# Value sums in the rotating PSUM banks, and ScalarE as a second copier, in an attention-plus-MLP kernel

## The chip, the cores and the metric

The kernel runs on one core of a Trainium2 chip. The metric is the device time of one execution in microseconds (us), as the median of several; lower is better. The five engines are called as in the profile: PE (TensorE, matrix products), DVE (VectorE), ACT (ScalarE), POOL (GpSimd) and SP (which issues most DMAs). "The skill" below always means the Trainium skill, named with the page.

## The reference, cut to what matters

```python
x = A_x                                      # (1, 2048, 512), bf16
xn = _layernorm(x)
return x + attention(xn, wqkv, wo) + mlp(xn, w_gate, w_up, w_down)

# attention: 32 heads of 16; causal, window of 256 keys
scores = einsum("bhqd,bhkd->bhqk", q, k) * (Dh ** -0.5)
p = softmax(where(mask, scores, -1e9));  o = einsum("bhqk,bhkd->bhqd", p, v);  o @ wo
# mlp, F = 1792:
h = (xn @ w_gate) * (xn @ w_up);  h @ w_down
```

## The kernel before

The 2048 positions are worked in four chunks (0 to 3) of 512. For a chunk there are 16 or 20 "steps": a step puts the scores of some heads into the PSUM tile `S` (four of the eight banks, one buffer), ACT takes the exp to `P`, and POOL and DVE mask `P`. Two steps later the value products of finished heads are summed, divided by the softmax sum on DVE, and turned into `OT`. Between the steps PE is filled with dense work in 512-column matmuls: the Q, K and V projections, gate and up of the MLP, and `down` and `wo` of the chunk before, whose sums share one PSUM bank. PE's program is one fixed sequence, so any late copy out of PSUM shows up as a wait of PE.

```python
self.ps_s = pool("ps_s", 1, space=PSUM)    # S: four banks
self.ps_a = pool("ps_a", 1, space=PSUM)    # the value sums' own bank, zeroed once
self.ps_m = pool("ps_m", 3, space=PSUM)    # three banks for all dense work
...
def zero_halves(self, j):                  # half-empty copies of V for half blocks
    for h in (0, 1) if j == 0 else (1,):
        self.nc.gpsimd.memset(self.Vh[j][h][64 - 64 * h:128 - 64 * h], 0.0)
...
def values(self, T, c, par):
    acc = self.accb
    ...
        for e in range(4):                 # four heads, one per column tile of PE
            nc.tensor.matmul(acc[32 * e:32 * e + 17, q:q + n],
                             lhsT=V[:, v, 8 * c + 2 * e + par, 0:17],     # 16 of V, one of ones
                             rhs=P[:, e, col:col + n], ..., tile_position=(0, 32 * e))
    nc.vector.transpose(out=at..., in_=acc[:])
    nc.vector.reciprocal(out=rz[:], in_=at[:, :, 16])
...
def gate(self, T, f, ks):
    ...
    nc.vector.tensor_copy(out=self.gsb[:], in_=ps[:])        # K and Q likewise on DVE
def up(self, T, f, ks):
    ...
    nc.vector.tensor_tensor(out=self.hT[T][:, f, :], in0=ps[:], in1=self.gsb[:], op=ALU.mult)
...
# fillers, chunk T:  each (cost, f, before, after); `after`: not before that step is divided
for b in range(4):
    down(T - 1, b)
    wo(T - 1, b, (0, 1))
    wo(T - 1, b, (2, 3))
    add(0, lambda T=T, b=b: self.store(T - 1, b))
...
self.wo(T, 3, (0, 1, 2, 3))                # the very end
self.store(T, 3, 1, True)                  # ACT's half of the last block
self.store(T, 3, 0)                        # DVE's half
```

The softmax here doesn't subtract the row's maximum and nothing guards it: scores larger than these inputs give would overflow.

Of the kernel before, what the change touches and what calls it, by code (L numbers as in the profile page):

```python
# [7 lines left out]
BF16 = mybir.dt.bfloat16  # L8
# [6 lines left out]

EVEN, ODD, PLAIN = 0, 1, 2
BIG = 2.0 ** 126


class Kernel:  # L20
    def __init__(self, ctx, tc, x, wqkv, wo, wg, wu, wd, out):
        self.tc, self.nc = tc, tc.nc
        _, S, D = x.shape
        self.S, self.D, self.F = S, D, wg.shape[1]
        assert D == 512 and S % 512 == 0 and self.F % 256 == 0
        self.NT, self.NCH, self.NF = S // 128, S // 512, self.F // 128
        self.x_d, self.out_d = x.flatten_outer_dims(), out.flatten_outer_dims()
        self.w_d = dict(qkv=wqkv, o=wo, g=wg, u=wu, d=wd)

        def pool(name, bufs, **kw):  # L30
            return ctx.enter_context(tc.tile_pool(name=name, bufs=bufs, **kw))

        self.const = pool("const", 1)
        self.chunk2 = pool("chunk2", 2)
        self.chunk3 = pool("chunk3", 3)
        self.ppool = pool("ppool", 6)
        self.work = pool("work", 2)
        self.xpool = pool("xpool", 4)
        self.small = pool("small", 4)
        self.ypool = pool("ypool", 4)  # L40
        self.ps_s = pool("ps_s", 1, space=bass.MemoryType.PSUM)
        self.ps_a = pool("ps_a", 1, space=bass.MemoryType.PSUM)
        self.ps_m = pool("ps_m", 3, space=bass.MemoryType.PSUM)


    def setup(self):
# [30 lines left out]
        nc.gpsimd.affine_select(out=ident[:], in_=ident[:], compare_op=ALU.not_equal, fill=1.0,  # L77
                                base=0, pattern=[[-1, 128]], channel_multiplier=1)
        self.ident = ident
        self.accb = self.ps_a.tile([128, 512], F32, name="accb")  # L80
        nc.vector.memset(self.accb[:], 0.0)
        wps = self.ps_m.tile([128, 128], F32, tag="M", name="wps")
        for _ in range(42):
            nc.tensor.matmul(wps[:], lhsT=ident[:], rhs=ident[:], start=True, stop=True)
# [16 lines left out]
        nc.gpsimd.memset(self.diag[64:128, 0, :], 0.0)  # L101
        self.xnT, self.Q, self.hT, self.O, self.OT = {}, {}, {}, {}, {}
        self.K, self.Ko, self.V = {}, {}, {}
        Vu, Vl0, Vl1 = (const.tile([128, 4, 32, 18], BF16, name=n) for n in ("Vu", "Vl0", "Vl1"))
        self.Vh = ((Vu, Vl0), (Vu, Vl1))
        self.strips, self.at = {}, {}

    def new_chunk(self, T):

        self.Q[T] = self.chunk2.tile([128, 4, 512], BF16, tag="Q", name=f"Q{T}")  # L110
        self.K[T] = self.chunk3.tile([128, 4, 512], BF16, tag="K", name=f"K{T}")
        self.Ko[T] = self.chunk3.tile([128, 4, 512], BF16, tag="Ko", name=f"Ko{T}")
        self.V[T] = self.chunk3.tile([128, 4, 32, 18], BF16, tag="V", name=f"V{T}")
        self.nc.gpsimd.memset(self.V[T][:, :, :, 16:18], 1.0)

    def zero_halves(self, j):

        for h in (0, 1) if j == 0 else (1,):
            self.nc.gpsimd.memset(self.Vh[j][h][64 - 64 * h:128 - 64 * h], 0.0)

    def copy_halves(self, T):

# [55 lines left out]
    def proj_v(self, t, ks=range(4)):  # L178
        nc = self.nc
        T, b = divmod(t, 4)  # L180
        ps = self.bank(ks, "vp")
        for k in ks:
            nc.tensor.matmul(ps[:], lhsT=self.xnT[T][:, b, k, :],  # L183
                             rhs=self.Wqkv[:, k, 1024:1536], start=(k == 0), stop=(k == 3))
        if 3 not in ks:
            return
        nc.scalar.activation(out=self.V[T][:, b, :, 0:16], in_=ps.rearrange("p (h d) -> p h d", h=32),  # L187
                             func=ACT.Copy)

    def proj_qk(self, T, c, is_k, ks=range(4), on_act=False):  # L190
        nc = self.nc
        lo = 512 * is_k + 128 * c
        ps = self.bank(ks, "qkp")
        for k in ks:
            nc.tensor.matmul(ps[:], lhsT=self.Wqkv[:, k, lo:lo + 128], rhs=self.xnT[T][:, :, k, :],  # L195
                             start=(k == 0), stop=(k == 3))
        if 3 not in ks:
            return
        if is_k:
            nc.vector.tensor_copy(out=self.K[T][:, c, :], in_=ps[:])  # L200
            nc.vector.tensor_scalar(out=self.Ko[T][:, c, :], in0=self.K[T][:, c, :],
                                    scalar1=self.odd[:, 0:1], scalar2=None, op0=ALU.mult)
        elif on_act:
            nc.scalar.activation(out=self.Q[T][:, c, :], in_=ps[:], func=ACT.Copy)
        else:
            nc.vector.tensor_copy(out=self.Q[T][:, c, :], in_=ps[:])

    def first_chunk(self):

        self.new_chunk(0)  # L210
        for b in range(2):
            self.norm_stats(b, 1)
            self.norm_scale(b, 1)
        for b in range(4):
            self.norm_apply(b)
            if b < 2:
                self.norm_stats(b + 2, 1)
                self.norm_scale(b + 2, 1)
        self.norm_transpose(0, False)
        for b in range(4):  # L220
            if b < 3:
                self.norm_transpose(b + 1, False)
            self.proj_v(b)
        self.zero_halves(0)
        self.proj_qk(0, 0, 1)
        self.proj_qk(0, 0, 0, on_act=True)
        self.proj_qk(0, 1, 1)
# [79 lines left out]
    def values(self, T, c, par):  # L307


        nc = self.nc  # L310
        acc = self.accb
        todo = []
        for kind, p in self.batches(T):
            if p in (par, None):
                P = self.strips.pop((T, c, kind, par))
                todo += [(P, *v) for v in self.value_pieces(T, kind, par)]
        for i, (P, col, h, kb, q, n) in enumerate(todo):
            U, v = divmod(4 * T + kb, 4)
            V = self.V[U] if h == 2 else self.Vh[U % 2][h]
            for e in range(4):  # L320
                nc.tensor.matmul(acc[32 * e:32 * e + 17, q:q + n],  # L321
                                 lhsT=V[:, v, 8 * c + 2 * e + par, 0:17],
                                 rhs=P[:, e, col:col + n], start=(i == 0), stop=(i == len(todo) - 1),
                                 tile_position=(0, 32 * e), skip_group_check=True)

        at = self.work.tile([128, 16, 32], F32, tag="at", name="at")
        nc.vector.transpose(out=at.rearrange("p b r -> p (b r)"), in_=acc[:])  # L327
        rz = self.small.tile([128, 16], F32, tag="rz")
        nc.vector.reciprocal(out=rz[:], in_=at[:, :, 16])
        self.at[(T, c, par)] = at, rz  # L330
# [16 lines left out]
    def gate(self, T, f, ks):  # L347
        nc = self.nc
        if f == 0 and 0 in ks:
            self.hT[T] = self.const.tile([128, self.NF, 512], BF16, tag="hT", name=f"hT{T}")  # L350
        ps = self.bank(ks, "gp")
        for k in ks:
            nc.tensor.matmul(ps[:], lhsT=self.Wg[:, k, 128 * f:128 * f + 128], rhs=self.xnT[T][:, :, k, :],  # L353
                             start=(k == 0), stop=(k == 3))
        if 3 not in ks:
            return
        self.gsb = self.work.tile([128, 512], BF16, tag="gsb", name="gsb")
        nc.vector.tensor_copy(out=self.gsb[:], in_=ps[:])  # L358

    def up(self, T, f, ks):  # L360
        nc = self.nc
# [128 lines left out]

    def run(self):
        self.xns, self.stats, self.sums = {}, {}, {}
        self.setup()
        NCH, LAG = self.NCH, 2
        RESERVE = 38
# [10 lines left out]
        SCORES, VALUES = 1.85, 3.5  # L506
        work = self.fillers()
        total = sum(w[0] for w in work) - RESERVE + SCORES * len(steps) + VALUES * (len(due) - 1)
        spent, n = 0, 0
        valued = -1  # L510

        def fill(upto, group):
            nonlocal spent, n
            while n < len(work):
                cost, f, before, after = work[n]
                if after is not None and after > valued:
                    break
                if spent + cost / 2 > upto and not any(
                        w[2] is not None and w[2] <= group for w in work[n:]):
                    break  # L520
                f()
                spent += cost
                n += 1
# [7 lines left out]
            return True  # L531

        def divide(g):
            nonlocal valued
            self.divide(*due[g])
            valued = g

        for g, s in enumerate(steps):
            fill(-1, g)
            self.scores(*s)  # L540
            spent += SCORES
            upto = total * (g + 1) / len(steps)
            if values(g - LAG):
# [11 lines left out]
        fill(spent + 10, -1)  # L555
        values(len(steps) - 1)
        divide(len(steps) - 1)
        fill(spent + 12, -1)
        for b in range(3):
            self.wo(T, b, (3,))  # L560
# [1 line left out]
        fill(10 ** 9, -1)  # L562
        assert n == len(work)
        self.wo(T, 3, (0, 1, 2, 3))
        self.store(T, 3, 1, True)
        self.store(T, 3, 0)


@with_exitstack
# [34 lines left out]
```

## Time and profile before

| | before |
|---|---|
| median of the runs | 279.75 us |
| span in the trace | 277.5 us |
| busy: PE, DVE, ACT, POOL | 264.6, 213.7, 156.4, 125.1 us |
| all waits of PE in the waits view, but "issue" | 6.4 us |

The head of the page of the kernel before gives for each engine the busy time, its share of the span and the number of instructions:

```profile
span 277.5 us, 10475 instructions
PE 264.6 (95%) x4697; PEld 128.7 (46%) x4718; DVE 213.7 (77%) x410; ACT 156.4 (56%) x101; POOL 125.1 (45%) x291
```

PE is the engine that bounds the kernel. A busy PE can still hide short waits, because matmul ends are modelled; so I also measured the gaps between the starts of successive dense matmuls, which follow each other at 216 ns when nothing is in the way. (A gap longer by exactly one matmul is a missing record. The "issue" lines below are such gaps: the trace has 4697 matmul records for 4718 weight loads.)

The waits view of the kernel before, for PE, says what ended its idle time; the columns are total us, number of times, and the longest:

```profile
PE xTp L169 <- DVE xn L153: 2.0, 2, 1.6
PE psd L381 <- issue: 1.6, 10, 0.2
PE wps L84 <- POOL ident L77: 1.4, 1, 1.4
PE psd L387 <- DVE OT L343: 1.1, 1, 1.1
PE up L364 <- DVE gsb L358: 1.0, 2, 0.8
PE psd L387 <- issue: 0.5, 3, 0.2
PE vp L183 <- ACT V L187: 0.3, 1, 0.3
PE gp L353 <- DVE hT L368: 0.3, 1, 0.3
PE qkp L195 <- ACT V L187: 0.3, 1, 0.3
```

No wait is large. Those for `xn`, `OT`, `gsb`, `hT` and `V` are what a change of this kind can reach. The largest has a cause that the timeline of the kernel before shows (start, duration, engine, line, operation, tiles, and in brackets the idle time before it):

```profile
8.21 2.19 DVE L153 TENSOR_SCALAR xn<-x,mv,rs 128x512 bf16<-128x512 bf16 x1 [0.77 <-POOL rs L145]
8.23 2.01 POOL L119 MEMSET Vu<- 64x2304 bf16 x1
...
10.45 0.34 PE L169 MATMUL xTp<-ident,xn 128*128 128x128 bf16 x3 [1.64 <-DVE xn L153]
```

The DVE operation takes 0.41 us elsewhere; here it ends 0.16 us after the POOL memset, and PE waits for it.

### The profile page before, as it was taken

How to read it: one execution, taken by the hardware profiler on the slowest of the kernel's cores; microseconds unless marked ns; L12 is line 12 of the kernel's file. 1: busy time of each engine (PE TensorE's matmuls, PEld its weight loads, DVE VectorE, ACT ScalarE, POOL GpSimd, SP SyncE). 2: the span in 40 equal slices, each digit the busy share in tenths (PEclk: the TensorE clock that was granted, in tenths of full speed). 3: DMA queues.
4: the chain of work that ended last, by engine and by line, in shares of the span. 5: the costliest groups of instructions: out<-in, count | busy, mean ns of one | idle time of the engine just before them, and what ended most of it. 6: DMA issues, size and time to landing. Idle time of an engine off the chain costs nothing.

```text
span 277.5 us, 10475 instructions
## 1 busy us (share of the span) xinstructions
PE 264.6 (95%) x4697; PEld 128.7 (46%) x4718; DVE 213.7 (77%) x410; ACT 156.4 (56%) x101; POOL 125.1 (45%) x291
## 2 busy tenths in 40 slices
PE   7799999899899999999999999999999999999994
PEld 6344444344344444444544444444444444444453
DVE  6489999959966989885986888885994569888332
ACT  3565555586456565567666655568755566655501
POOL 6715535446647244353446635242543524254400
PEclk9999999999999999999999999999999999999999
DMA  6999411200031100000002210000000100000002
GB/s 196 379 372 349 131 21 21 21 2 2 2 78 40 40 5 2 2 2 2 2 20 61 57 23 4 0 5 2 2 2 21 40 19 5 2 4 2 2 0 78
DMA packets 17180, 14.04 MB, mean 51 GB/s; under 512 B 7024, under 2 KB 17136, under 8 KB 17136
## 3 DMA queue, kind: packets, MB, share of 16 engines
q1 hardware_dynamic: 16848, 13.18, 15.8%
q8 instruction: 37, 0.61, 0.9%
q10 hardware_dynamic: 288, 0.20, 0.2%
q14 instruction: 7, 0.06, 0.1%
HBM read 9.70 MB, written 2.10 MB: 43 GB/s over the span
## 4 chain that ended last, share of the span: by engine, by line
PE 79%; DVE 13%; issue 2%; ACT 2%; DMA 1%; POOL 1%; DVEq 0%; ACTq 0%
PE psd L381 17%; PE up L364 15%; PE gp L353 14%; PE qkp L195 11%; PE S L263 9%; PE accb L321 8%; PE psd L387 4%; PE vp L183 3%; DVE gsb L358 2%; DVE hT L368 2%; DVE xn L153 2%; DVE st L134 2%; DVE at L327 1%; ACT P L269 1%; DVE OT L343 1%
## 5 line engine op out<-in xcount | busy, mean ns | idle before, releaser
L269 ACT ACTIVATE P<-S 128x2048 bf16<-128x2048 f32 x76 | 142.6, 1877 | 98.2 <-PE S L263 74.6
L277 POOL TENSOR_SCALAR_AFFINE_SELECT P<-P 128x256 bf16<-128x256 bf16 x112 | 49.5, 462 | 126.0 <-ACT P L269 126.0
L364 PE MATMUL up<-xnT,Wu 128*128 128x512 bf16 x224 | 59.3, 380 | 1.1 <-DVE gsb L358 1.0
L353 PE MATMUL gp<-xnT,Wg 128*128 128x512 bf16 x224 | 59.7, 380 | 0.3 <-DVE hT L368 0.3
L281 POOL TENSOR_SCALAR_AFFINE_SELECT P<-P 128x256 bf16<-128x256 bf16 x128 | 56.0, 460 | 0.0
L381 PE MATMUL psd<-Wd,hT 128*128 128x512 bf16 (+1 forms) x224 | 51.5, 366 | 1.8 <-issue 1.6
L368 DVE TENSOR_TENSOR hT<-up,gsb 128x512 bf16<-128x512 f32 x56 | 38.1, 681 | 6.5 <-PE up L364 4.4
L358 DVE CAST gsb<-gp 128x512 bf16<-128x512 f32 x56 | 37.9, 677 | 3.6 <-PE gp L353 3.6
L327 DVE STREAM_TRANSPOSE at<-accb 128x512 f32<-128x512 f32 x32 | 22.9, 716 | 16.8 <-PE accb L321 16.3
L292 DVE TENSOR_TENSOR P<-P,diag 128x512 bf16<-128x512 bf16 x64 | 29.1, 455 | 6.2 <-ACT P L269 6.1
L381 PEld LDWEIGHTS <-hT 128*128 128x128 bf16 x238 | 21.9, 98 | 23.2 <-issue 0.2
L364 PEld LDWEIGHTS <-Wu 128*128 128x128 bf16 x224 | 20.4, 98 | 25.9 <-issue 2.2
L353 PEld LDWEIGHTS <-Wg 128*128 128x128 bf16 x224 | 20.1, 98 | 24.2 <-issue 0.9
L195 PE MATMUL qkp<-xnT,Wqkv 128*128 128x512 bf16 x128 | 30.4, 380 | 0.3 <-ACT V L187 0.3
L321 PE MATMUL accb<-P,V 128*17 128x64 bf16 (+2 forms) x960 | 26.1, 220 | 0.0
L321 PE MATMUL accb<-P,Vu 128*17 128x64 bf16 x512 | 20.7, 193 | 0.0
L321 PEld LDWEIGHTS <-V 128*17 128x17 bf16 x960 | 17.1, 92 | 4.9 <-issue 0.4
L321 PE MATMUL accb<-P,Vl 128*17 128x64 bf16 x448 | 18.9, 193 | 0.0
L405 DVE TENSOR_TENSOR y<-psd,x 128x512 bf16<-128x512 f32 (+1 forms) x15 | 9.9, 667 | 11.5 <-PE psd L387 9.2
L200 DVE CAST K<-qkp 128x512 bf16<-128x512 f32 x16 | 10.9, 682 | 10.1 <-PE qkp L195 10.1
L195 PEld LDWEIGHTS <-Wqkv 128*128 128x128 bf16 x128 | 11.6, 98 | 14.6 <-issue 1.4
L387 PE MATMUL psd<-Wo,OT 128*128 128x512 bf16 (+1 forms) x65 | 16.5, 366 | 1.6 <-DVE OT L343 1.1
(51 smaller groups left out, 233.7 us busy)
## 6 DMA issues: line engine op xcount, KB each, us to landing
Wg<-in_B_w_gate_dram SPq DMA_DIRECT2D x2, 896.0 KB, 11.0
Wu<-in_B_w_up_dram SPq DMA_DIRECT2D x2, 896.0 KB, 11.8
Wd<-in_B_w_down_dram SPq DMA_DIRECT2D x1, 1792.0 KB, 15.0
out_dram<-y SPq DMA_DIRECT2D x14, 128.0 KB, 1.7
Wqkv<-in_A_wqkv_dram SPq DMA_DIRECT2D x3, 512.0 KB, 6.8
x<-in_A_x_dram SPq DMA_DIRECT2D x1, 1024.0 KB, 10.4
x<-in_A_x_dram SPq DMA_DIRECT2D x1, 512.0 KB, 11.6
Wo<-in_A_wo_dram SPq DMA_DIRECT2D x1, 512.0 KB, 14.9
```

Source lines behind the costliest of these rows:

```text
L195: nc.tensor.matmul(ps[:], lhsT=self.Wqkv[:, k, lo:lo + 128], rhs=self.xnT[T][:, :, k, :], start=(k == 0), stop=(k == 3))
L269: nc.scalar.activation(out=P[:], in_=S[:], func=ACT.Exp, scale=0.25)
L277: nc.gpsimd.affine_select(out=P[:, :, col:col + 64], in_=P[:, :, col:col + 64], pattern=[[0, 4], [-1, 64]], compare_op=ALU.is_gt, fill=0.0 ...
L281: nc.gpsimd.affine_select(out=P[:, :, col:col + 64], in_=P[:, :, col:col + 64], pattern=[[0, 4], [1, 64]], compare_op=ALU.is_ge, fill=0.0, ...
L292: self.nc.vector.tensor_tensor(out=both, in0=both, op=ALU.min, in1=m.unsqueeze(1).to_broadcast([128, 4, 2, 64]))
L321: nc.tensor.matmul(acc[32 * e:32 * e + 17, q:q + n], lhsT=V[:, v, 8 * c + 2 * e + par, 0:17], rhs=P[:, e, col:col + n], start=(i == 0), st ...
L353: nc.tensor.matmul(ps[:], lhsT=self.Wg[:, k, 128 * f:128 * f + 128], rhs=self.xnT[T][:, :, k, :], start=(k == 0), stop=(k == 3))
L358: nc.vector.tensor_copy(out=self.gsb[:], in_=ps[:])
L364: nc.tensor.matmul(ps[:], lhsT=self.Wu[:, k, 128 * f:128 * f + 128], rhs=self.xnT[T][:, :, k, :], start=(k == 0), stop=(k == 3))
L368: nc.vector.tensor_tensor(out=self.hT[T][:, f, :], in0=ps[:], in1=self.gsb[:], op=ALU.mult)
L381: nc.tensor.matmul(ps, lhsT=self.hT[T][:, f, 128 * b:128 * b + 128], rhs=self.Wd[:, f, c0:c1], start=(f == 0), stop=False)
L387: self.nc.tensor.matmul(ps, lhsT=self.OT[T][:, c, 128 * b:128 * b + 128], rhs=self.Wo[:, c, c0:c1], start=False, stop=(c == 3))
```

## The change

Its intent: share the bank that was kept for the value sums, so that all work outside `S` takes turns on four banks. For this the value matmuls write all 32 rows of their quarter of the bank (V weights of 32 columns, the last 15 being ones, other heads' data or padding that nobody reads), so no bank has to be zeroed and reserved. ACT takes the K, Q and gate copies that come due when its exp should be over (by the program's own count, after 11 units of PE work since the scores, a unit being one dense matmul). The zeroing of the first two V halves moves from POOL to ACT. `wo` is let loose one step later, and the last two stores change places.

```diff
+VW = 4 * 32 * 18 + 16
+ACT_FREE = 11
-        self.ps_a = pool("ps_a", 1, space=bass.MemoryType.PSUM)
-        self.ps_m = pool("ps_m", 3, space=bass.MemoryType.PSUM)
+        self.ps_m = pool("ps_m", 4, space=bass.MemoryType.PSUM)
-        self.accb = self.ps_a.tile([128, 512], F32, name="accb")
-        nc.vector.memset(self.accb[:], 0.0)
 ... (setup)
+        nc.vector.memset(self.zero[:], 0.0)
+        self.zero_halves(0)
 ... (zero_halves)
+        for h in range(2):
+            rows = slice(64 - 64 * h, 128 - 64 * h)
+            self.nc.scalar.activation(out=self.Vh[0][h][rows],
+                                      in_=self.zero[rows].to_broadcast([64, VW]), func=ACT.Copy)
 ... (K; Q and the gate copy gsb likewise)
-            nc.vector.tensor_copy(out=self.K[T][:, c, :], in_=ps[:])
+            if self.act_free:
+                nc.scalar.activation(out=self.K[T][:, c, :], in_=ps[:], func=ACT.Copy)
+            else:
+                nc.vector.tensor_copy(out=self.K[T][:, c, :], in_=ps[:])
 ... (values)
-        acc = self.accb
+        acc = self.ps_m.tile([128, 512], F32, tag="M", name="acc")
-                nc.tensor.matmul(acc[32 * e:32 * e + 17, q:q + n],
-                                 lhsT=V[:, v, 8 * c + 2 * e + par, 0:17],
+                at = 18 * (32 * v + 8 * c + 2 * e + par)
+                nc.tensor.matmul(acc[32 * e:32 * e + 32, q:q + n], lhsT=V[:, at:at + 32],
 ... (run: fill)
+                self.act_free = spent + cost - scored >= ACT_FREE    # PE work since the scores
                 f()
 ... (run: divide, and the loop over steps)
-            valued = g
+            ready = g
+            valued = ready        # at the start of the next step
 ... (the end)
-        self.store(T, 3, 1, True)
         self.store(T, 3, 0)
+        self.store(T, 3, 1, True)
```

More of the change, by code (lines that the diff above doesn't have):

```diff
@@ L103, in setup @@
         self.K, self.Ko, self.V = {}, {}, {}
-        Vu, Vl0, Vl1 = (const.tile([128, 4, 32, 18], BF16, name=n) for n in ("Vu", "Vl0", "Vl1"))
+        Vu, Vl0, Vl1 = (const.tile([128, VW], BF16, name=n) for n in ("Vu", "Vl0", "Vl1"))
         self.Vh = ((Vu, Vl0), (Vu, Vl1))
+        self.zero = const.tile([128, 1], BF16, name="zero")
+        nc.vector.memset(self.zero[:], 0.0)
+        self.zero_halves(0)
         self.strips, self.at = {}, {}
@@ L112, in new_chunk, with heads @@
         self.Ko[T] = self.chunk3.tile([128, 4, 512], BF16, tag="Ko", name=f"Ko{T}")
-        self.V[T] = self.chunk3.tile([128, 4, 32, 18], BF16, tag="V", name=f"V{T}")
-        self.nc.gpsimd.memset(self.V[T][:, :, :, 16:18], 1.0)
-    def zero_halves(self, j):
-        for h in (0, 1) if j == 0 else (1,):
-            self.nc.gpsimd.memset(self.Vh[j][h][64 - 64 * h:128 - 64 * h], 0.0)
+        self.V[T] = self.chunk3.tile([128, VW], BF16, tag="V", name=f"V{T}")
+        self.nc.gpsimd.memset(self.heads(self.V[T])[:, :, :, 16:18], 1.0)
+        self.nc.gpsimd.memset(self.V[T][:, VW - 16:], 0.0)
+    def heads(self, V):
+        return V[:, 0:VW - 16].rearrange("p (b h d) -> p b h d", b=4, h=32)
+    def zero_halves(self, j):
+        if j:
+            self.nc.gpsimd.memset(self.Vh[1][1][0:64], 0.0)
+            return
+        for h in range(2):
+            rows = slice(64 - 64 * h, 128 - 64 * h)
+            self.nc.scalar.activation(out=self.Vh[0][h][rows],
+                                      in_=self.zero[rows].to_broadcast([64, VW]), func=ACT.Copy)
     def copy_halves(self, T):
@@ L186, in proj_v @@
             return
-        nc.scalar.activation(out=self.V[T][:, b, :, 0:16], in_=ps.rearrange("p (h d) -> p h d", h=32),
+        nc.scalar.activation(out=self.heads(self.V[T])[:, b, :, 0:16], in_=ps.rearrange("p (h d) -> p h d", h=32),
                              func=ACT.Copy)
@@ L199, in proj_qk @@
         if is_k:
-            nc.vector.tensor_copy(out=self.K[T][:, c, :], in_=ps[:])
+            if self.act_free:
+                nc.scalar.activation(out=self.K[T][:, c, :], in_=ps[:], func=ACT.Copy)
+            else:
+                nc.vector.tensor_copy(out=self.K[T][:, c, :], in_=ps[:])
             nc.vector.tensor_scalar(out=self.Ko[T][:, c, :], in0=self.K[T][:, c, :],
                                     scalar1=self.odd[:, 0:1], scalar2=None, op0=ALU.mult)
-        elif on_act:
+        elif on_act or self.act_free:
             nc.scalar.activation(out=self.Q[T][:, c, :], in_=ps[:], func=ACT.Copy)
@@ L223, in first_chunk @@
             self.proj_v(b)
-        self.zero_halves(0)
         self.proj_qk(0, 0, 1)
@@ L357, in gate @@
         self.gsb = self.work.tile([128, 512], BF16, tag="gsb", name="gsb")
-        nc.vector.tensor_copy(out=self.gsb[:], in_=ps[:])
+        if self.act_free:
+            nc.scalar.activation(out=self.gsb[:], in_=ps[:], func=ACT.Copy)
+        else:
+            nc.vector.tensor_copy(out=self.gsb[:], in_=ps[:])
     def up(self, T, f, ks):
@@ L492, in run @@
         self.xns, self.stats, self.sums = {}, {}, {}
+        self.act_free = False
         self.setup()
@@ L508, in run @@
         total = sum(w[0] for w in work) - RESERVE + SCORES * len(steps) + VALUES * (len(due) - 1)
-        spent, n = 0, 0
-        valued = -1
+        spent, n, scored = 0, 0, 0
+        valued, ready = -1, -1
         def fill(upto, group):
@@ L533, in divide @@
         def divide(g):
-            nonlocal valued
+            nonlocal ready
             self.divide(*due[g])
-            valued = g
+            ready = g
         for g, s in enumerate(steps):
             fill(-1, g)
+            valued = ready
             self.scores(*s)
+            scored = spent
             spent += SCORES
@@ L557, in run @@
         divide(len(steps) - 1)
+        valued = ready
         fill(spent + 12, -1)
@@ L564, in run @@
         self.wo(T, 3, (0, 1, 2, 3))
+        self.store(T, 3, 0)
         self.store(T, 3, 1, True)
-        self.store(T, 3, 0)
 @with_exitstack
```

## The prediction

> **What bounds it now.** PE. The page gives PE 264.6 of 277.5 us busy (95%), DVE 213.7 (77%), ACT 156.4 (56%); the chain of waits is 79% PE. Dense 512-column matmuls start 216 ns apart. So only PE's stalls and the two ends can be won. The waits view lists PE stalls of 9.2 us in all; from start-to-start gaps (slightly more than the idle shown) the real ones are:
> - 1.8 us at 8.6 us: the fourth xTp waits for xn, whose DVE op took 2.19 us instead of 0.41, from 8.21 us, beside a POOL memset of the V halves from 8.23 for 2.01 us. The Trainium skill, "SBUF — State Buffer" (Who interferes with whom), says that a VectorE 2-port op and GpSimd exclude each other for a whole instruction; this trace agrees.
> - 1.8 us in chunk 0 (0.44, 0.39, 0.95 near 36, 37, 50 us): gate/up banks wait for DVE, 44.8 of 49 us busy from 19 to 68.
> - 1.3 us at 73.7: wo waits for the DVE transpose OT.
> - 0.45, 0.42, 0.3 at 57, 127, 93 us: banks waiting for ACT's V copies or a DVE copy.
>
> **What the change does.** By the instruction order PE executes the same sequence; only four matmuls of one step (chunk 1, the wo that waited 1.3 us) move behind the next scores.
>
> 1. Zeroing of the first two halves goes from POOL (2 x 2.0 us) to ACT. Estimate from exp (2048 elements 1.88 us) and V copy (512, 0.60): 2.1 us each, so ACT is free at about 6.5 us; the first xnT copy wants it at 6.04: +0.5 against -1.8. Net -1.3 us.
> 2. 37 of DVE's PSUM copies (0.68 us) go to ACT (0.60): DVE -25 us, ACT +22 (+4 for zeroing). A moved copy falls at least 2.4 us after its scores, when exp (0.36 + 1.88) is done; the next scores come 3.2 us after the last. So exp should rarely be late.
> 3. Four shared banks instead of 3+1; values hold one for 0.8 us plus a 0.72 us transpose, otherwise dense work has it. With 2, chunk-0 stalls fall by 1.5 us, later ones by 0.8.
> 4. wo a step later: -1.3 us, but that step becomes 2.0 us of PE work against exp's 2.3: about 0.4 comes back. Net -0.9.
> 5. Last store: DVE's half no longer waits 2.3 us for ACT's: -0.4 us.
>
> Added: V weights of 32 columns instead of 17. The column tiles start a 64-column piece every 29 ns. The Trainium skill, "TensorE: Matmul & The Clock Gate" (LDWEIGHTS), has load time columns/1.2 ns: 27 ns for 32, just fitting. The trace shows 92 ns latency for 17 columns and 104 for 64, so I estimate +4 ns, hidden. If not, some 370 groups each pay.
>
> **Sum.** -1.3 -1.5 -0.8 -0.9 -0.4 = -4.9 us, plus 0.4 for new ACT waits: -4.5. Predicted 275.3 us (range 273.8 to 278.0), 1.6% faster. Chances: faster by over 2% 0.14, within 2% 0.81, slower 0.05.
>
> **What would show it.** The fourth xn at 0.41 us, the stall before the fourth xTp under 0.3 us, first scores 1.3 us earlier; DVE busy near 189 us, ACT 182; PE waits on gsb, hT and OT nearly gone; 64-column value pieces still 29 ns apart, a value stage still 0.79 us.
>
> **What would make it wrong.** Wider V loads stretching the value stage (26 ns each would cost 10 us); acc waiting for a bank that a slow ACT copy holds; ACT's zeroing delaying the first chunk more than the stall it removes; exps delayed by copies so that PE waits before scores.

## The result, and the profile after

| | before | after |
|---|---|---|
| median | 279.78 us (279.68 to 279.81, 4 runs) | 274.74 us (274.64 to 274.85, 4 runs) |
| span in the trace | 277.5 us | 272.9 us |
| start of PE's last matmul | 273.45 us | 268.49 us |
| DVE, ACT busy | 213.7, 156.4 us | 193.9, 178.9 us |

The ratio of the two is 0.982, with a 95% interval of 0.980 to 0.984: 1.8% less. A ratio is the mean time of one kernel's fast runs over that of the other's of the same rounds, so it is not quite the ratio of the medians quoted.

The head of the page of the changed kernel:

```profile
span 272.9 us, 10526 instructions
PE 263.3 (96%) x4697; PEld 129.7 (48%) x4718; DVE 193.9 (71%) x376; ACT 178.9 (66%) x137; POOL 122.8 (45%) x293
```

PE has the same number of matmuls on record and is busy 1.3 us less; the span is 4.6 us shorter. So at least 3.3 us of what went is idle time; the 1.3 us can be waits too, which modelled ends count as busy. The waits view of the changed kernel, for PE:

```profile
PE psd L397 <- issue: 1.6, 10, 0.2
PE wps L83 <- POOL ident L78: 1.4, 1, 1.4
PE S L276 <- ACT P L282: 0.8, 1, 0.8
PE psd L403 <- issue: 0.5, 3, 0.2
PE xTp L180 <- DVE xn L164: 0.4, 1, 0.4
PE vp L194 <- ACT xnT L181: 0.3, 1, 0.3
```

The waits for `gsb`, `hT`, `OT` and `V` are gone; two new ones have come, 0.8 us of the scores for an exp and 0.3 us for `xnT`. The timeline of the changed kernel at its beginning shows both the cure and the price of the zeroing:

```profile
2.31 2.13 ACT L129 ACTIVATE Vu<-zero 64x2320 bf16<-64x2320 bf16 x1
...
4.45 2.14 ACT L129 ACTIVATE Vl<-zero 64x2320 bf16<-64x2320 bf16 x1
...
6.49 1.05 ACT L181 ACTIVATE xnT<-xTp 128x512 bf16<-128x512 bf16 x2
...
7.12 1.04 PE L194 MATMUL vp<-Wqkv,xnT 128*128 128x512 bf16 x3 [0.28 <-ACT xnT L181]
...
8.33 0.41 DVE L164 TENSOR_SCALAR xn<-x,mv,rs 128x512 bf16<-128x512 bf16 x1 [0.77 <-POOL rs L156]
```

ACT is busy zeroing until 6.49 us, so the first `xnT` is late and PE waits 0.28 us; but the fourth `xn` takes 0.41 us instead of 2.19.

Since PE's sequence is the same in both but for one step, the starts of the 76 score stages can be laid side by side. The shift changes only at a few places:

| place (time in the kernel before) | shift of the score starts, after minus before |
|---|---|
| first scores (15.1 us) | -1.12 us |
| steps 7, 9, 11 (38, 45, 52 us), gate and up of chunk 0 | -0.82, -0.10, -1.01 |
| steps 13, 15, 17 (59, 65, 72 us), V and Q, K of chunk 1 | -0.45, -0.20, -0.09 |
| step 18 and 19 (76, 79 us), the wo that waited for OT | -1.33, then +0.90 |
| steps 24, 34, 55 (95, 128, 196 us) | -0.36, -0.41, -0.08 |
| PE's last matmul, all together (the places add up to -5.07, the rest is drift) | -4.96 |
| from there to the end of the span (4.08 us before, 4.39 after) | +0.31 |

That leaves 0.4 us between the 4.65 us of the span and the 5.04 us of the medians, outside what the trace covers.

### The profile page after: what moved, and what is told of

The parts are those of the page before. It is cut to its first block, busy times and chain, and to the rows that moved or that the text cites. A ratio compares the mean times of both kernels' runs of the same rounds, so it can differ in the third digit from the quotient of the medians.

```text
span 272.9 us, 10526 instructions
## 1 busy us (share of the span) xinstructions
PE 263.3 (96%) x4697; PEld 129.7 (48%) x4718; DVE 193.9 (71%) x376; ACT 178.9 (66%) x137; POOL 122.8 (45%) x293
## 4 chain that ended last, share of the span: by engine, by line
PE 93%; ACT 4%; issue 1%; POOL 1%; DVE 0%; ACTq 0%
PE gp L366 19%; PE up L380 18%; PE psd L397 17%; PE qkp L206 10%; PE S L276 10%; PE acc L335 9%; PE vp L194 5%; PE psd L403 5%; ACT P L282 1%; ACT Vl L129 1%; ACT Vu L129 1%; ACT L75 0%; POOL P L290 0%; POOL P L294 0%; ACT xnT L181 0%
## 5 line engine op out<-in xcount | busy, mean ns | idle before, releaser
L282 ACT ACTIVATE P<-S 128x2048 bf16<-128x2048 f32 x76 | 142.7, 1877 | 59.7 <-PE S L276 40.1
L340 DVE STREAM_TRANSPOSE at<-acc 128x512 f32<-128x512 f32 x32 | 22.9, 716 | 23.4 <-PE acc L335 23.2
L305 DVE TENSOR_TENSOR P<-P,diag 128x512 bf16<-128x512 bf16 x64 | 31.4, 490 | 7.0 <-ACT P L282 6.9
L335 PE MATMUL acc<-P,V 128*32 128x64 bf16 (+2 forms) x960 | 26.3, 221 | 0.0
L374 DVE CAST gsb<-gp 128x512 bf16<-128x512 f32 x33 | 22.4, 677 | 2.6 <-PE gp L366 1.8
L372 ACT ACTIVATE gsb<-gp 128x512 bf16<-128x512 f32 x23 | 13.7, 597 | 12.7 <-PE gp L366 12.7
L335 PE MATMUL acc<-P,Vu 128*32 128x64 bf16 x512 | 20.7, 193 | 0.0
L335 PEld LDWEIGHTS <-V 128*32 128x32 bf16 x960 | 17.9, 97 | 4.9 <-issue 0.4
L335 PE MATMUL acc<-P,Vl 128*32 128x64 bf16 x448 | 19.0, 193 | 0.0
L276 PE MATMUL S<-Q,K 16*64 16x64 bf16 (+3 forms) x896 | 17.2, 236 | 0.9 <-ACT P L282 0.8
L276 PEld LDWEIGHTS <-K 16*64 16x64 bf16 (+1 forms) x896 | 8.3, 103 | 19.4 <-issue 19.4
```

What stands on the lines that cost most here:

```text
L276: nc.tensor.matmul(S[outs, e, col:col + n], lhsT=(self.Ko if p else self.K)[U][rows, c, keys], rhs=self.Q[T][rows, c, q:q + n], start=True ...
L282: nc.scalar.activation(out=P[:], in_=S[:], func=ACT.Exp, scale=0.25)
L305: self.nc.vector.tensor_tensor(out=both, in0=both, op=ALU.min, in1=m.unsqueeze(1).to_broadcast([128, 4, 2, 64]))
L335: nc.tensor.matmul(acc[32 * e:32 * e + 32, q:q + n], lhsT=V[:, at:at + 32], rhs=P[:, e, col:col + n], start=(i == 0), stop=(i == len(todo) ...
L340: nc.vector.transpose(out=at.rearrange("p b r -> p (b r)"), in_=acc[:])
```

## The experiments

Each is the changed kernel with one edit, unless said otherwise. "PE's end" is the start of its last matmul against the changed kernel's 268.49 us; it is free of what happens after PE's work, which turned out to matter.

### 1. Zeroing back on POOL

```diff
-        self.zero_halves(0)                   # in setup, on ACT
...
-            self.nc.scalar.activation(out=self.Vh[0][h][rows], ...)
+            self.nc.gpsimd.memset(self.Vh[0][h][rows], 0.0)
...
+        self.zero_halves(0)                   # after the V projections, as before
```

> The changed kernel with the zeroing of the first two V halves back on POOL, in its old place after the V projections; all else as changed. My theory (a POOL memset holds the SBUF port pair and the fourth xn op waits for it): the fourth xn takes about 2.2 us again instead of 0.41, the fourth transpose on PE waits 1.7 us, the first scores start 1.1 us later (15.1 instead of 13.98) and the whole kernel is 1.1 us slower, 275.85 against 274.74. Rival (the start gained because the DVE memset of the bank went and the copies of Q moved): xn stays at 0.41 us and the time stays at 274.7.

Measured: 275.53 us (275.52 to 275.56), first scores at 15.21 us, 1.23 later, and PE's end 1.23 later. Its timeline:

```profile
8.31 2.20 DVE L162 TENSOR_SCALAR xn<-x,mv,rs 128x512 bf16<-128x512 bf16 x1 [0.76 <-POOL rs L154]
8.33 2.03 POOL L128 MEMSET Vu<- 64x2320 bf16 x1
```

The `xn` operation takes 2.20 us again, beside a memset of 2.03 us. The theory holds and the rival falls: neither the memset of the bank nor the Q copies had anything to do with the start. The skill, "SBUF — State Buffer" (Who interferes with whom), gives a mechanism that fits: DVE in a 2-port mode and POOL share one pair of ports, "Whoever issues first gets the shared pair for the whole instruction; the other fully blocks (not throttle)". The trace agrees in length: the operation took 1.79 us longer than 0.41 and ended 0.15 us after the memset. That it runs in a 2-port mode no trace here shows. Moving the zeroing to ACT, which by the same page has ports of its own, freed DVE. The whole kernel lost only 0.79 us where PE's end lost 1.23: 0.26 us of the difference is in the end of the program (experiment 4), the other 0.2 outside what the trace covers.

### 2. Which of the two removed the waits in the middle: banks or copies?

Four kernels make a square: the changed one; without the copies on ACT; without the shared bank; without either.

```diff
-ACT_FREE = 11
+ACT_FREE = 10 ** 6                            # no copies on ACT by position
```

> The changed kernel with no K, Q or gate copy moved to ScalarE by position; the four shared banks stay. PE's stalls between 33 us and 130 us lost 3.6 us in the change (0.82 + 0.10 + 1.01 + 0.45 + 0.20 + 0.09 in chunk 0 and its end, 0.36 + 0.41 + 0.08 later, by the shift of the score starts). Theory A, a fourth bank lets PE run past a late copy: at least 2.5 us of the 3.6 stay gained, time 274.7 to 275.8. Theory B, it is DVE's load that counts (DVE 44.8 of 49 us busy there before): the stalls of 0.4 to 1.0 us near 33 and 48 us come back, time about 277.

```diff
-        self.ps_m = pool("ps_m", 4, space=bass.MemoryType.PSUM)
+        self.ps_a = pool("ps_a", 1, space=bass.MemoryType.PSUM)
+        self.ps_m = pool("ps_m", 3, space=bass.MemoryType.PSUM)
...
-        acc = self.ps_m.tile([128, 512], F32, tag="M", name="acc")
+        acc = self.accb                       # from ps_a
```

> The changed kernel with the value sums in a bank of their own and three banks for dense work, as before; the copies on ScalarE stay. Theory A (fourth bank): most of the 3.6 us come back, time about 277. Theory B (DVE's load): the gate and up stalls stay gone, only V copies (0.45 us at the end of chunk 0, 0.4 us later) wait again, time 275 to 275.8.

Both edits together:

> Both undone: three banks plus one and no copies moved to ScalarE; zeroing on ScalarE, the later wo and the store order stay. Both theories: the whole 3.6 us return, time about 278.3; if it is well below that, part of the gain in the middle came from something else, such as the later wo.

The first of them was run twice, since its profile fell in a disturbed execution (see the last section):

> The same kernel as in the run without copies on ScalarE, once more, because its profile fell in an execution in which every dense matmul took over twice its time (666 us). Expected: 275.63 us again in the fast state, and a profile that shows where its 0.9 us over the changed kernel lie: by my reading (four banks let PE run ahead, but DVE is still the only copier), stalls of gate and up for DVE in chunk 0 between 33 and 55 us, smaller than the 0.4 to 1.0 us of the kernel before, and none or 0.1 us after 90 us.

| | copies on ACT | no copies on ACT |
|---|---|---|
| four shared banks | 274.74 us (changed kernel) | 275.63 and, again, 275.66 us |
| three and one | 276.20 us | 278.02 us |

By time the fourth bank alone takes away 278.02 - 275.63 = 2.4 us, the copies alone 278.02 - 276.20 = 1.8 us, both together 3.3 us. By PE's end it is 2.2, 2.0 and 3.6 us. (The second and third figures differ from those by time through the program's end, experiment 4; the first through 0.19 us at the start of the trace with banks only, where PE waited 0.5 us for weights from a DMA.) So neither theory won: each edit alone gives over half of the gain, and together they give less than the sum, because some waits fall to either. The expectation for the time of the kernel with banks only was met, though 2.2 us stayed gained by PE's end (2.4 without the wait at the start) and not 2.5; that for the kernel with copies only lay on both sides of what came. With neither, 278.3 us was expected and 278.02 came. Against the kernel before, the score starts of this one differ by more than 0.06 us from step to step only at the start and at the `wo` of steps 18 and 19, so nothing else in the change worked on the waits in the middle. (The 3.6 us of the expectation are 3.5 by its own bracket.)

The shifts tell which wait fell to what. Each cell is how much the lag of the score starts behind the changed kernel grows at that place:

| place | neither | banks only | copies only |
|---|---|---|---|
| steps 7 to 12, gate and up of chunk 0 | +1.91 | +1.18 | +0.55 |
| step 13, four V copies on ACT | +0.45 | 0 | +0.46 |
| steps 15 and 17 | +0.30 | 0 | 0 |
| step 24, gate copy | +0.36 | 0 | 0 |
| step 34, V copies again | +0.41 | 0 | +0.42 |

The waits view of the kernel with banks only has what is left for DVE:

```profile
PE gp L366 <- DVE gsb L374: 0.7, 1, 0.7
PE up L380 <- DVE gsb L374: 0.2, 1, 0.2
```

that with copies only has the waits for V:

```profile
PE vp L196 <- ACT V L200: 0.3, 1, 0.3
PE qkp L208 <- ACT V L200: 0.3, 1, 0.3
PE up L382 <- DVE gsb L376: 0.2, 1, 0.2
```

and that with neither has both, as the kernel before had:

```profile
PE up L382 <- DVE gsb L376: 1.0, 2, 0.8
PE vp L196 <- ACT V L200: 0.3, 1, 0.3
PE gp L368 <- DVE hT L386: 0.3, 1, 0.3
PE qkp L208 <- ACT V L200: 0.3, 1, 0.3
```

The two edits complement each other. The V copies run on ACT in both kernels, and four come due behind one exp of 1.88 us; only a fourth bank lets PE go on meanwhile. In chunk 0, DVE is the late copier (44.8 of 49 us busy from 19 to 68 us before). As I read it, a fourth bank only lets PE run one group further there before it waits; taking copies off DVE does more (0.55 us left against 1.18). The skill, "TensorEngine Tiling (Array Packing)" (PSUM Bottleneck), advises to "Use both ScalarE and VectorE for PSUM evacuation"; here that is worth 0.9 us on top of the fourth bank, and 1.8 us without it.

### 3. Does it matter that the copies fall between the exps?

```diff
-ACT_FREE = 11
+ACT_FREE = 0                                  # ACT takes every K, Q and gate copy
```

> The changed kernel with the placement rule taken away: ScalarE takes every K, Q and gate copy, also those that come due right after the scores and so stand behind or before an exp. Theory (the place between exps matters): exps start up to 0.6 us later and copies wait up to 1.9 us behind an exp, so PE waits before scores or for gate copies, and the time is 276 us or more although DVE is relieved by another 20 us. Rival (four banks hide the place; only the sum of the load counts, and ScalarE at about 205 of 273 us is still below PE): the time stays within 0.4 us of 274.74.

Measured: 274.46 us (274.39 to 274.53), 0.3 us faster than the changed kernel. PE's end is the same within 0.08 us, so PE gained nothing; the 0.3 us are again in the end of the program. The head of its page:

```profile
PE 263.9 (97%) x4697; PEld 130.1 (48%) x4718; DVE 161.0 (59%) x325; ACT 201.9 (74%) x188; POOL 120.7 (44%) x293
```

DVE fell by another 33 us and ACT rose by 23, and no wait of PE for a copy came. The rival holds: with four banks, the rule that places the copies between the exps is not needed. Whether it would matter with three banks was not run.

### 4. The later wo, and the end

`wo` let loose at once, as before:

```diff
-            ready = g
+            ready = valued = g
```

> The changed kernel with the output projection freed as soon as the division is issued, as before, instead of a step later. In the changed kernel PE waits 0.8 us (0.94 by starts) for the exp of the short step near 69.6 us; before, it waited 1.3 us there for the transpose OT. My theory: OT's chain on DVE (transpose, reciprocal, multiply, transpose: 2.1 us at least after the value stage) does not get shorter with less DVE load, so the 1.3 us wait is back and the 0.94 us wait is gone: 0.4 us slower, about 275.15. Rival: with DVE less loaded, OT comes in time, and without the short step the kernel is 0.5 to 0.9 us faster, about 274.0.

Measured: 275.09 us (275.08 to 275.09), PE's end 0.44 us later. The wait for `OT` is back at its old length although DVE is less loaded:

```profile
71.16 0.39 PE L403 MATMUL psd<-Wo,OT 128*128 128x512 bf16 x1 [1.15 <-DVE OT L356]
```

The theory holds: in that trace the four DVE operations behind `OT` follow each other without other work, from 68.89 to 71.10 us, so less load on DVE cannot shorten them. What the later `wo` gains is 1.34 - 0.90 = 0.44 us.

The single matmuls show where these 0.44 us come from. The `wo` matmul that needs the last part of `OT` starts at 71.16 us in both kernels, right after `OT` is done at 71.10. The weight load for it (PEld is PE's loading of weights) waits for `OT` in the changed kernel too:

```profile
71.16 0.10 PEld L403 LDWEIGHTS <-OT 128*128 128x128 bf16 x1 [0.15 <-DVE OT L356]
```

So `OT` still sets the pace. The later `wo` only lets PE do the next scores before that matmul and not after it, and these take 0.43 us of PE's time (in the trace with `wo` at once, 71.60 to 72.25 us between the starts of two dense matmuls, less the usual 0.22). The changed kernel waits for an exp in the same stretch:

```profile
70.58 0.29 PE L276 MATMUL S<-Q,K 16*128 16x128 bf16 x8 [0.78 <-ACT P L282]
```

This wait costs nothing of its own. In the kernel with banks only the exp came earlier, but then PE waited for `OT`, as two lines of its waits view say:

```profile
PE S L276 <- ACT P L282: 0.5, 1, 0.5
PE psd L403 <- DVE OT L356: 0.2, 1, 0.2
```

By the next score start it had lost again the 0.30 us that it was ahead. The kernels with neither, with zeroing on POOL and with zeroing on DVE do the same. Why the exp starts 0.87 us after its scores in the changed kernel (68.65 against 67.78) and 0.56 us in these stays open; the copies on ACT are not the reason, since zeroing on POOL has them too.

The old order of the last two stores:

```diff
-        self.store(T, 3, 0)
         self.store(T, 3, 1, True)
+        self.store(T, 3, 0)
```

> The changed kernel with the last stores in their old order, ScalarE's half first. From PE's last matmul start to the end the span has 4.4 us in the changed kernel and 4.05 before, so the new order seems to have lost about 0.35 us where I predicted a gain of 0.4: the two halves' reads of one PSUM tile follow each other in both orders, and now ScalarE's DMA issue comes last. My theory: 0.35 us faster, about 274.4. Rival: the end is longer for another reason (the time the DMA takes from run to run) and the time stays within 0.1 of 274.74.

Measured: 274.66 us (274.62 to 274.71), within 0.1 us. My theory fell. In either order the second half waits for the first (0.42 us on DVE, 0.38 on ACT), and SP's last wait for the stores ends 2.95 us (old order) or 2.97 us (new) after PE's last matmul start. The order is worth nothing. The 0.31 us by which the span's end was longer lie after that, between the end barrier's events: from PE's last matmul start to the end of the span it takes 4.08 to 4.13 us in the kernel before, in that with zeroing on POOL, in that with banks only (second run), in that with neither and in that where ACT takes all; and 4.35 to 4.39 us in all others. No edit that I can name sorts them. The cause stays open, and a difference of 0.3 us between two of these kernels' times need not be one in work.

### 5. A better order for wo

With four banks two sums can be open at once. So the first block's second half of `wo` can stand behind the next block's `down`:

```diff
                     down(T - 1, b)
                     wo(T - 1, b, (0, 1))
-                    wo(T - 1, b, (2, 3))
-                    add(0, lambda T=T, b=b: self.store(T - 1, b))
+                    if b == 0:
+                        continue
+                    for late in (0, 1) if b == 1 else (b,):
+                        wo(T - 1, late, (2, 3))
+                        add(0, lambda T=T, b=late: self.store(T - 1, b))
```

> The changed kernel with the second half of the first block's wo after the next block's down sums in every chunk, so that PE has work of its own while OT is made. It needs two open sums at once, which four banks allow. My theory: the short step near 69 us is full again, PE's 0.8 us wait for exp goes and no OT wait comes back: 0.9 us faster, about 273.85. Rival: a bank wait replaces it (two sums and the value sum hold three of four banks), and the time stays.

Measured: 273.77 us (273.77 to 273.86), ratio to the kernel before 0.979 (0.977 to 0.980), which counts as unclear, since the interval holds the threshold of 2%. PE's end is 0.80 us earlier, the shift at that step 0.90. PE's timeline there has `down` work where the wait was:

```profile
69.28 0.59 PE L403 MATMUL psd<-Wo,OT 128*128 128x512 bf16 x2
69.72 1.03 PE L397 MATMUL psd<-Wd,hT 128*128 128x512 bf16 x4
70.67 0.29 PE L276 MATMUL S<-Q,K 16*128 16x128 bf16 x8
```

The theory holds; no wait for a bank came.

### 6. Zeroing on DVE in its own gap

DVE has nothing to do from 8.7 to 12.4 us.

```diff
-            self.nc.scalar.activation(out=self.Vh[0][h][rows], ...)
+            self.nc.vector.memset(self.Vh[0][h][rows], 0.0)             # and called after the V projections
```

> The changed kernel with the first two V halves zeroed by DVE after its last xn, in a gap of 3.6 us that the trace shows there (8.7 to 12.4 us). My theory: it costs DVE about 1.5 us of the gap (a DVE copy of the same size takes 0.75 us) and nothing else, and ScalarE is free for the first xnT at 6.07 us instead of 6.49, so PE's 0.28 us wait for it goes: first scores 0.2 to 0.5 us earlier, time about 274.4. Rival: the first chunk is then held by something else (weights from DMA, the V copies on ScalarE), no gain.

Measured: 274.52 us, but from 274.35 to 274.83; first scores in the one trace at 14.17 us, 0.19 later. Inconclusive. Together with the better order of wo:

> The reordered wo together with the zeroing on DVE. With the zeroing on DVE the first scores came no earlier in one look (14.17 against 13.98 us), and the median was 0.2 us lower with a spread as large. If that was chance, this runs like the reordered wo alone, 273.8; if the zeroing on DVE is worth 0.2 us, 273.55.

Measured: 273.63 us in two groups, 273.41 and 273.43, and 273.84 and 273.92; ratio to the kernel before 0.978 (0.977 to 0.980). In its trace the first scores came at 13.65 us, 0.33 earlier than in the changed kernel. A difference between the two traces fits the two groups. In the first (274.83 us, the highest of its kernel) the first four transposes on PE start within 0.32 us and are done at 6.51 us, and the first `xnT` starts at 6.55; the trace's record of PE's clock goes to full at 7.47 us. In the second (273.43 us, nearly the lowest) they start within 0.18 us and are done at 5.76 us, and `xnT` starts at 5.79; the clock goes to full at 4.68 us. I read it so: ACT is now free in time, and whether that helps depends on how early PE's clock comes up. Two traces don't show it. This is the fastest kernel, by a hair.

## Why the prediction was right or wrong, point by point

The time was predicted as 275.3 us in a range of 273.8 to 278.0, and was 274.74. The ground of the prediction, that PE's sequence stays and only its waits go, held. By terms:

- **The start: -1.3 predicted, -1.12 measured** (1.23 in experiment 1). Right in mechanism and nearly in size; ACT was free at 6.49 us, as estimated (6.5).
- **Banks and copies: -2.3 predicted (-1.5 and -0.8), -3.4 measured** (-0.82 - 0.10 - 1.01 - 0.45 - 0.20 - 0.09 - 0.36 - 0.41). Right in mechanism, too small in size: I left part of each wait standing, and none stayed; and I had not counted the waits at steps 9, 15 and 17. That the two edits overlap in some waits and complement each other in others I had not seen.
- **Copies moved: 37 predicted, 34 measured** (23 gate, 7 more Q, 4 K). DVE fell by 19.8 us instead of 25, ACT rose by 22.5 instead of 26.
- **wo a step later: -0.9 predicted, -0.43 measured.** This step was wrong in part. I took the 1.3 us wait for `OT` as gone and only an exp's 0.4 as coming back. But `OT` still sets the pace (experiment 4): its last `wo` matmul starts at 71.16 us in either order, and the gain is just the time of the scores that moved before it. That the exp came later than I reckoned (0.87 us after its scores, not 0.36) made no difference: the kernels in which it came after 0.56 us gain nothing by it.
- **The last store: -0.4 predicted, +0.31 measured.** This step was wrong. I took DVE's listed wait for ACT as time lost, but the two halves follow each other in either order (experiment 4), so nothing was to be had; and the end barrier took 0.3 us more, which nothing in the profile before announced.
- **New waits for ACT: +0.4 predicted.** Two were seen: 0.28 us for `xnT`, counted in the start, and 0.78 us for the exp of the short step, which cost nothing of its own.
- **V weights of 32 columns: nothing predicted, +0.17 us measured.** See below.

The terms predicted too large (start, wo, store: 0.2 + 0.5 + 0.7 us) and those predicted too small (banks and copies 1.1, ACT waits 0.4) cancel nearly, which is luck; the total is closer than its parts. Nothing that was to make the prediction wrong came: no wait of a value sum for a bank, no delay before scores but one.

The value stages, by the groups view, first of the kernel before and then of the changed one (busy us and mean ns after the first bar, idle after the second):

```profile
L321 PEld LDWEIGHTS <-V 128*17 128x17 bf16 x960 | 17.1, 92 | 4.9 <-issue 0.4
```

```profile
L335 PEld LDWEIGHTS <-V 128*32 128x32 bf16 x960 | 17.9, 97 | 4.9 <-issue 0.4
```

A load takes 5 ns more, as estimated (4). The mean spacing of 64-column pieces on a column tile went from 29.3 to 29.5 ns, and the 32 value stages together from 26.22 to 26.39 us. So nearly all of the longer load is hidden. By the skill's rule of columns/1.2 ns, "TensorE: Matmul & The Clock Gate" (LDWEIGHTS), my estimate for 15 more columns would have been 12.5 ns (the prediction's 27 ns for 32 columns is an estimate by the same rule).

## What to carry to other kernels

When the busiest engine runs one fixed sequence, lay the starts of its stages side by side before and after: the shift grows only where a wait went, and each place can be given its cause. A spare PSUM bank and a second engine that empties banks are two cures for overlapping sets of waits: try each alone, because the bank helps where one engine's copies come in a burst and the second engine helps where the first is loaded all the time. A producer chain with a fixed length (here the four operations to `OT`) is not cured by freeing its engine, and a later place for the consumer gains only as much as the work that moves before it; put other work of the waiting engine in between.

## What the Trainium skill lacked or had wrong

- "SBUF — State Buffer" (Who interferes with whom) says that whoever issues first gets the shared ports for the whole instruction. In the trace DVE's `xn` starts 0.02 us before the POOL memset (8.21 against 8.23 us, and 8.31 against 8.33 in experiment 1), and it is DVE that takes 1.78 us longer. Both wait for the same POOL operation before, and the profile calls POOL's times rough; so a start in the trace does not tell who holds the ports.
- "TensorE: Matmul & The Clock Gate" (LDWEIGHTS) gives columns/1.2 ns. At full clock, loads of 17, 32 and 64 columns were recorded with 92, 97 and 104 ns (the 64 are those of the scores), but loads of 128 columns with 92 to 98 ns. So the recorded time does not follow the columns. Most of it is a latency that overlaps, since the value pieces start every 29 ns; the rate itself no run here isolates.
- The same page (Seeing it yourself) says of the trace's clock events that they can be unreliable, and of the throttle that it has been seen stuck. One execution of the kernel with banks only took 668 us, with three others at 275.6: dense matmuls started 621 ns apart at the median instead of 216, and exps took their usual 1877 ns. Its trace holds no clock event at all, so the clock of 1.00 that is listed for it says nothing. What slowed PE is not known.
- That the end of a program can take two lengths is on no page that I found (it would belong to "Runtime: NRT & Kernel Launch"). The stretch after PE's last matmul took either about 4.1 or about 4.37 us in the one fast trace looked at of each kernel, with the last store's wait ending at the same 2.95 to 2.98 us in all.
